# One explicit order of single-engine pieces for the first stage of an attention, MoE and MLP kernel

## The chip, the core and the metric

The kernel runs on one core of a Trainium2 chip. A core has five engines that run side by side, each with its own instruction list in fixed order: PE (TensorE, the matmuls; PEld is its weight load), DVE (VectorE), ACT (ScalarE), POOL (GpSimd) and SP (SyncE, which here only issues DMAs). They wait for each other through semaphores. SBUF is the on-chip memory of 128 partitions; PSUM takes the results of PE. The metric is the device time of one execution in microseconds (us), the median of several runs.

## The reference

```
def _attn_ref(q, k, v, n_global, n_local):
    scores = scale * np.matmul(q, k.transpose(0, 1, 3, 2))
    ...
    scores = np.where(keep, scores + bias, -1e9)   # local window and a few global keys
    a = np.exp(scores - max); a = a / (sum(a) + 1e-09)
    return np.matmul(a, v)

def _moe_ref(x, w_in, w_out, g_ln):
    h = x @ w_in
    e = np.exp(h - max(h)); sm = e / (sum(e) + 1e-09)
    solu = h * sm
    ln = (solu - mean) / np.sqrt(var + 1e-06) * g_ln
    return ln @ w_out

def _moe2_ref(x, w_in, w_out):
    h = x @ w_in
    return (h * (1.0 / (1.0 + np.exp(-h)))) @ w_out
```

Attention has 2 batches, 8 heads, 768 positions and heads of 64; n_global is 8 and n_local 96. Its output, 1536 tokens by 512, goes through the first block (512 to 1024 to 512) and the second (512 to 2048 to 512). The weights arrive as 64-bit floats.

## The kernel before

**Tiles and stages.** The tokens are cut into 12 tiles of 128, six to a batch. The first stage takes each tile through attention and the first block; its result lies transposed in x2T (128 partitions, 4 parts of the model width, 1536 tokens). The second stage takes two groups of 768 tokens through the second block: `up` (L485) and `down` (L512), 16 steps each, interleaved by one.

A tile's chain in the first stage: scores of 8 heads in two groups of four (`scores`, L248); per head the maximum with the bias on DVE (L264), which leaves the biased scores in a tile A and the maximum in negmax, and the exponential on ACT (L265), which also sums into sm; per group the reciprocals of the sums on DVE (L270, L271); a scaling of A by head (`norm`, L115 through the helper `scaled`) on POOL or DVE; eight transposes (L285) and a copy out to ath; the product with v (L304), which lands as a high part xT on ACT (L324) and a low part on DVE (L329); two halves of the product with w_in (L343). Then a softmax times h and a layernorm in pieces lm, le, lu, ls, sq, lc, ld (L353 to L388, the last a scaling of e on POOL), transposes of e (L398), high and low part lnh on ACT (L402) and lnl on DVE (L405), and the product with w_out (L418) for pairs of tiles in two halves, copied to x2T (L428, L430). Tiles of the first position of a batch (0 and 6) have a window of 128 keys, the others 256.

**High and low parts.** Products with weights are made of three: high by high, low by high and high by low. A weight therefore needs a high part and the remainder, and is unpacked first from its 64-bit form, in 48 units of 128x512: load (`cl`, L108, 512 KB, into cx), exponent scaling into cc (`ca`, `cap`, `cav` for ACT, POOL, DVE; L113 or L115), three bit operations on DVE (c1, c2, c3: L128, L130, L132), for w_out a scaling with the gain g_ln (L141, two instructions on POOL), the high copy (L113 on ACT, L115 on DVE) and the subtraction of the low part (L143, POOL). Units 0 to 7 are w_in, 8 to 15 w_out, 16 to 47 the second block.

**Order.** Nothing is scheduled by a compiler: each engine's list is the order in which the program calls the pieces. For tiles 0 to 7 a string START of tokens such as `ea:0` gives it, for tiles 8 to 11 the string STEADY is repeated with the tile number relative, then LAST, and a tail in Python with the first two `up` steps. One token covers several instructions, often on several engines: `ea` is the maxima of two heads on DVE and their exponentials on ACT, `na` and `nb` are the sums of one group (DVE) and its four norms, divided among POOL and DVE by the digit, `cs` is gain, high and low part of a unit. In the repeated part and behind it, `bg` runs a unit's next steps, one unit behind the other. All DMAs are issued by SP.

**Buffers.** cx and cc have 3 buffers, sm 3, st 2 and xT 2 (LEAD). The outputs of `down` are copied from PSUM into a pool tile ob of 6 buffers and sent from there (L519 to L524).

Of the kernel before, what the change touches and what calls it, by code (L numbers as in the profile page):

```python
# [8 lines left out]
F32 = mybir.dt.float32  # L9
# [36 lines left out]
def kernel(ctx, tc, q, k, v, n_global, n_local, w_in, w_out, g_ln, w2_in, w2_out, out):  # L46
# [58 lines left out]
    def u_load(i):  # L105
        src, b, _, _ = units[i]
        x = cv.tile([128, 512, 2], I32, tag="cx", name="cx", bufs=3)
        nc.sync.dma_start(out=x.rearrange("p (b n) t -> p b n t", b=b) if b else x, in_=src)  # L108
        ustate[i] = [x]
# [24 lines left out]
    def u_split(i, eng=None, heng=None):  # L134
        _, b, dest, g = units[i]
        hi, lo = dest()
        w = ustate.pop(i)[1]
        if b:
            w = w.rearrange("p (b n) -> p b n", b=b)
        for j in range(b if g is not None else 0):  # L140
            nc.gpsimd.tensor_scalar(out=w[:, j], in0=w[:, j], scalar1=g[:, j:j + 1], scalar2=1.0, op0=ALU.mult, op1=ALU.mult)  # L141
        scaled(hi, w, heng)
        (eng or nc.gpsimd).tensor_tensor(out=lo, in0=w, in1=f(hi), op=ALU.subtract)  # L143

    NW1 = 2 * KD + KF
    ustep = [NW1 - 3]
# [104 lines left out]
    def softmax(t, qd, j):  # L251
# [3 lines left out]
        if j == 0:  # L255
# [4 lines left out]
        for a in range(2):  # L260
            h, c = 4 * qd + 2 * j + a, 2 * a + j
            bb = bias[:, h, s:s + 2, :].rearrange("p w n -> p (w n)") if tb else bias0[:, h, :]
            m = negmax[:, t * H + h:t * H + h + 1]
            nc.vector.tensor_tensor_reduce(out=x[:, c, 0:n], in0=p[:, a, j, 0:n], in1=bb, scale=-0.125, scalar=1e30, op0=ALU.add, op1=ALU.min, accum_out=m)  # L264
# [570 lines left out]
```

## Time and profile before

| | us |
|---|---|
| median of 3 runs (lowest, highest) | 542.16 (541.45, 544.44) |
| the profiled execution | 541.32 |
| its span, first to last instruction | 539.2 |

| engine | busy us | share of the span | instructions |
|---|---|---|---|
| PE | 496.1 | 92% | 3025 |
| PEld | 436.4 | 81% | 3025 |
| DVE | 316.5 | 59% | 711 |
| ACT | 240.5 | 45% | 548 |
| POOL | 154.5 | 29% | 199 |

The mean granted TensorE clock was 0.988 of full speed. The same page shows the span in 40 slices of 13.5 us, each digit the busy share in tenths (row PEclk is the granted clock):

```profile
PE   1668778899999999989999999999999999999994
PEld 1345657788898889879989899898998999989893
DVE  4998989666645643673988889884263122131221
ACT  3656666456555654544564544543242222122221
POOL 1787885322144314341344333232000000000000
PEclk9998899999999999999999999999999999999997
```

The prediction reads three more views. In the table of windows, a row is a stretch of the span with the busy time of each engine, the granted clock and what the DMAs moved. In the chain of waits, a row is the start, the length and the work that the end of the span depended on at that time. In the groups of instructions, a row has a line, its engine, what it writes and reads with the shapes, the count, the busy time in us with the mean of one in ns, and behind the bar the idle time of the engine just before and what ended it. In the trace, matmuls of scores (L248) and with v (L304) are recorded twice each.

### The profile page before, as it was taken

The numbers are of one execution on the slowest core, as the hardware profiler recorded it, in microseconds if no ns is written. First come the engines' busy times: TensorE is split into PE (matmuls) and PEld (weight loads), VectorE is DVE, ScalarE is ACT, GpSimd is POOL, SyncE is SP. The second block draws the span as 40 slices with busy tenths as digits, with TensorE's granted clock in tenths as the row PEclk, the third lists the DMA queues.
The fourth block names the chain that finished last, engine by engine and source line by source line (L and its number), as shares of the span: only waits on it lengthen the run. The fifth ranks groups of instructions, "written<-read, shape, count | busy, mean of one in ns | idle before, by whom it ended". The sixth has DMA issues, their size and how long they took to land.

```text
span 539.2 us, 8089 instructions
## 1 busy us (share of the span) xinstructions
PE 496.1 (92%) x3025; PEld 436.4 (81%) x3025; DVE 316.5 (59%) x711; ACT 240.5 (45%) x548; POOL 154.5 (29%) x199
## 2 busy tenths in 40 slices
PE   1668778899999999989999999999999999999994
PEld 1345657788898889879989899898998999989893
DVE  4998989666645643673988889884263122131221
ACT  3656666456555654544564544543242222122221
POOL 1787885322144314341344333232000000000000
PEclk9998899999999999999999999999999999999997
DMA  7575430202053000210253342420030000000003
GB/s 210 179 203 170 133 119 23 79 22 78 1 176 98 2 2 1 78 40 1 79 194 119 117 147 98 146 78 2 0 118 1 1 0 1 0 1 1 0 1 123
DMA packets 27487, 38.36 MB, mean 71 GB/s; under 512 B 2864, under 2 KB 15152, under 8 KB 27440
## 3 DMA queue, kind: packets, MB, share of 16 engines
q1 hardware_dynamic: 27440, 37.76, 22.2%
q8 instruction: 26, 0.43, 0.3%
q14 instruction: 21, 0.17, 0.1%
HBM read 34.61 MB, written 3.15 MB: 70 GB/s over the span
## 4 chain that ended last, share of the span: by engine, by line
PE 75%; DVE 9%; POOL 7%; DMA 3%; ACT 3%; issue 2%; SPq 0%; POOLq 0%; ACTq 0%
PE p L485 25%; PE p L512 25%; PE p L418 10%; PE p L343 7%; PE p L285 2%; PE p L248 2%; DMA cx<-in_moe_w_in_dram 2%; PE p L304 2%; PE p L398 2%; POOL A L115 2%; DVE cc L130 1%; DVE cc L132 1%; DVE A L264 1%; POOL cc L141 1%; ACT A L265 1%
## 5 line engine op out<-in xcount | busy, mean ns | idle before, releaser
L494 DVE SCALAR_TENSOR_TENSOR e<-e,p 128x384 f32<-128x384 f32 x64 | 32.6, 550 | 123.8 <-ACT e L491 123.8
L491 ACT ACTIVATE e<-p 128x384 f32<-128x384 f32 x64 | 27.9, 488 | 126.4 <-PE p L485 126.4
L512 PE MATMUL p<-w3h,gl 128*128 128x512 f32 x192 | 75.8, 395 | 0.0
L512 PE MATMUL p<-w3l,gh 128*128 128x512 f32 x192 | 75.7, 394 | 0.0
L512 PE MATMUL p<-w3h,gh 128*128 128x512 f32 x192 | 75.5, 393 | 0.0
L132 DVE SCALAR_TENSOR_TENSOR cc<-cx,cc 128x512 uint32<-128x512 uint32 x48 | 61.3, 1276 | 0.2
L485 PE MATMUL p<-x2h,w2h 128*128 128x384 f32 x256 | 55.6, 338 | 0.0
L485 PE MATMUL p<-x2l,w2h 128*128 128x384 f32 x256 | 55.5, 338 | 0.0
L485 PE MATMUL p<-x2h,w2l 128*128 128x384 f32 x256 | 55.4, 338 | 0.0
L343 PE MATMUL p<-wih,xT 128*128 128x512 f32 x192 | 50.9, 408 | 1.4 <-DVE xT L329 1.4
L265 ACT ACTIVATE A<-A,negmax 128x256 f32<-128x256 f32 (+1 forms) x96 | 45.9, 480 | 13.8 <-DVE negmax L264 12.4
L115 POOL TENSOR_SCALAR A<-A,sm 128x256 f32<-128x256 f32 (+1 forms) x63 | 33.4, 544 | 53.9 <-DVE sm L271 52.4
L485 PEld LDWEIGHTS p<-x2h,w2h 128*128 128x128 f32 x256 | 46.1, 188 | 2.6
L485 PEld LDWEIGHTS p<-x2l,w2h 128*128 128x128 f32 x256 | 46.0, 188 | 0.0
L485 PEld LDWEIGHTS p<-x2h,w2l 128*128 128x128 f32 x256 | 45.8, 188 | 0.0
L343 PEld LDWEIGHTS p<-wih,xT 128*128 128x128 f32 x192 | 35.1, 192 | 10.8 <-issue 1.8
L512 PEld LDWEIGHTS p<-w3h,gl 128*128 128x128 f32 x192 | 36.1, 188 | 8.3
L285 PE MATMUL p<-ident,A 128*128 128x128 f32 x176 | 27.4, 300 | 15.9 <-POOL A L115 15.8
L512 PEld LDWEIGHTS p<-w3l,gh 128*128 128x128 f32 x192 | 36.0, 188 | 7.3
L512 PEld LDWEIGHTS p<-w3h,gh 128*128 128x128 f32 x192 | 36.1, 188 | 7.1
L95 ACT ACTIVATE gh<-e 128x384 fp32r<-128x384 f32 x64 | 31.6, 526 | 20.7 <-DVE e L494 20.7
L130 DVE SCALAR_TENSOR_TENSOR cc<-cx,cc 128x512 uint32<-128x512 uint32 x48 | 39.8, 829 | 0.1
(101 smaller groups left out, 834.0 us busy)
## 6 DMA issues: line engine op xcount, KB each, us to landing
cx<-in_moe_w_in_dram SPq DMA_DIRECT2D x24, 512.0 KB, 3.7
cx<-in_moe_w_out_dram SPq DMA_DIRECT2D x24, 512.0 KB, 3.5
rq<-in_q_dram SPq DMA_DIRECT2D x12, 256.0 KB, 3.9
rk<-in_k_dram SPq DMA_DIRECT2D x12, 256.0 KB, 4.6
vf<-in_v_dram SPq DMA_DIRECT2D x12, 256.0 KB, 4.1
out_dram<-ob SPq DMA_DIRECT2D x12, 256.0 KB, 3.1
ints<-in_n_local_dram SPq DMA_DIRECT2D x1, 1.0 KB, 2.5
ints<-in_n_global_dram SPq DMA_DIRECT2D x1, 1.0 KB, 3.9
```

The costliest lines, as they stand in the source:

```text
L95: nc.scalar.activation(out=hi, in_=src, func=ACTF.Copy)
L115: eng.tensor_scalar(out=out, in0=in_, scalar1=scale, scalar2=1.0, op0=ALU.mult, op1=ALU.mult)
L130: V.scalar_tensor_tensor(out=y, in0=x[:, :, 0].bitcast(U32), scalar=29, in1=y, op0=ALU.logical_shift_right, op1=ALU.bitwise_or)
L132: V.scalar_tensor_tensor(out=y, in0=x[:, :, 1].bitcast(U32), scalar=0x80000000, in1=y, op0=ALU.bitwise_and, op1=ALU.bitwise_or)
L265: nc.scalar.activation(out=x[:, c, 0:n], in_=x[:, c, 0:n], func=ACTF.Exp, bias=m, scale=-1.0, accum_out=sm[:, 0, c:c + 1])
L285: nc.tensor.transpose(p[:, w, o:o + 128], x[:, c, w * 128:(w + 1) * 128], ident)
L343: nc.tensor.matmul(p[:, half, :], lhsT=x[:, a, kk, :], rhs=w[:, kk, n], start=(i == 0), stop=(i == 11))
L418: nc.tensor.matmul(p[:, d], lhsT=x[:, kk, c], rhs=y[:, kk, sl], start=(i == 0), stop=(i == 3 * KF - 1))
L485: nc.tensor.matmul(p, lhsT=w[m // 2][:, kk, c], rhs=x[:, kk, s * HG:(s + 1) * HG], start=(i == 0), stop=(i == 11))
L491: nc.scalar.activation(out=e, in_=p2[:, s, 0:HG], func=ACTF.Tanh, scale=0.5)
L494: nc.vector.scalar_tensor_tensor(out=E[s], in0=E[s], scalar=1.0, in1=p2[:, s, 0:HG], op0=ALU.add, op1=ALU.mult)
L512: nc.tensor.matmul(o, lhsT=x[:, c], rhs=w[m // 2][:, m % 2, :], start=(m == 0 and i == 0), stop=(last and i == 2))
```

## The change

START, STEADY, LAST and the tail give way to one string ORDER of 861 tokens, which covers the first stage from its first load to the last copy into x2T. Its tokens are pieces of one engine, and each names its engine where there is a choice: `d0` to `d7` is the maximum of one head (DVE, now L294), `x0` to `x7` the exponential of one head (ACT, L300), `ra` and `rb` the sums of a group (DVE, L304, L305), `m0p` or `m0v` the norm of one head on POOL or DVE, `oaa` or `oav` the copy out of transposes on ACT or DVE, `ugp`, `uha`, `ulp` (or with v) the gain, high and low part of a unit, `Y00v` one copy into x2T. The head of the table, and the pieces that the old tokens fall into:

```
ORDER = """
cl:0 lq:0 lk:0 cep:0 c1:0 ba:0 sb:0 bb:0 c2:0 cl:1 sa:0 c3:0 d0:0 d4:0 cep:1 d1:0 d5:0 d2:0 lk:1 d6:0 c1:1 d3:0 lq:1 kg:0 c2:1 bc:0 cl:2 d7:0 lq:2
...

-        x = cv.tile([128, 512, 2], I32, tag="cx", name="cx", bufs=3)
-        nc.sync.dma_start(out=x.rearrange("p (b n) t -> p b n t", b=b) if b else x, in_=src)
+        x = cv.tile([128, 512, 2], I32, tag="cx", name="cx", bufs=5)
+        (nc.sync if i else nc.scalar).dma_start(out=x.rearrange("p (b n) t -> p b n t", b=b) if b else x, in_=src)
...
-        c = cv.tile([128, 512], F32, tag="cc", name="cc", bufs=3)
+        c = cv.tile([128, 512], F32, tag="cc", name="cc", bufs=4)
...
-            sm = at.tile([128, 2, 4], F32, tag="sm", name="sm", bufs=3)
+            sm = at.tile([128, 2, 4], F32, tag="sm", name="sm", bufs=6)
...
-        x = m1.tile([128, 2, 4, 128], F32R, tag="xT", name="xT", bufs=LEAD)
+        x = at2.tile([128, 2, 4, 128], F32R, tag="xT", name="xT", bufs=3)
...
-        st = m1.tile([128, 8], F32, tag="st", name="st", bufs=2)
+        st = m1.tile([128, 8], F32, tag="st", name="st", bufs=3)
...
+    def u_gain(i, eng):
+        w, g = u_parts(i)[0], units[i][3]
+        for j in range(units[i][1]):
+            eng.tensor_scalar(out=w[:, j], in0=w[:, j], scalar1=g[:, j:j + 1], scalar2=1.0, op0=ALU.mult, op1=ALU.mult)
+
+    def u_hi(i, eng=None):
+        w, hi, _ = u_parts(i)
+        scaled(hi, w, eng)
+
+    def u_lo(i, eng):
+        w, hi, lo = u_parts(i)
+        eng.tensor_tensor(out=lo, in0=w, in1=f(hi), op=ALU.subtract)
+        ustate.pop(i)
...
-    ustep = [NW1 - 3]
+    NWA = NW1 + 8
+    ustep = [NWA]
...
+    def masks3():
         nc.vector.tensor_copy(bias[:, :, 2, :], bias[:, :, 0, :])
...
+    def snorm(t, i, eng):
+        n = 256 if t % TB else 128
+        qd, _, _, _, c = head(i)
+        x, sm, _ = A[t, qd]
+        scaled(x[:, c, 0:n], x[:, c, 0:n], eng, sm[:, 1, c:c + 1])
...
-                    y = wo.tile([128, DM], F32, tag="ob", name="ob", bufs=6)
+                    y = x2T[:, r // 384, r // 128 % 3 * DM:(r // 128 % 3 + 1) * DM]
...
-        nc.sync.dma_start(out=gt, in_=g_ln.rearrange("(k p) -> p k", p=128))
-        for x in START.split():
+        for x in ORDER.split():
...
+            if x == "lk:0":
+                nc.sync.dma_start(out=gt, in_=g_ln.rearrange("(k p) -> p k", p=128))
```

The pool wo is gone: a result of `down` is copied into a part of x2T that no later step reads, and sent from there. The units of the second block that `bg` runs in the second stage begin with unit 24 instead of continuing two units behind; the split of unit 23 falls into the second stage. The second stage's order is otherwise as it was, with `up` cut into its pieces.

Three places of the order, row by row.

PE around the first product with w_out. Before, the transposes of tile 2's e stand ahead of the first L418 (lnh, lnl by woh, wol), and six groups of products with w_in (L343, 12 matmuls each) lie ahead of these rows:

```order
L398 MATMUL p<-ident,e 128x128 x8
L285 MATMUL p<-ident,A 128x128 x8
L248 MATMUL p<-rk,rq 128x256 x4
L418 MATMUL p<-lnh,woh 128x256 x8
L418 MATMUL p<-lnh,wol 128x256 x8
L418 MATMUL p<-lnl,woh 128x256 x8
```

The first L398 of these rows is that of tile 1; the one of tile 2 stands fourteen rows on. In the changed kernel the same engine reads, with L380 for the products with w_in, L275 for scores, L341 for the product with v and L455 for that with w_out:

```order
L380 MATMUL p<-wil,xT 128x512 x4
L275 MATMUL p<-rk,rq 128x128 x4
L341 MATMUL p<-ath,vf 64x128 x16
L455 MATMUL p<-lnh,woh 128x256 x8
L455 MATMUL p<-lnh,wol 128x256 x8
L455 MATMUL p<-lnl,woh 128x256 x8
```

Ten groups of products with w_in now lie ahead of the first L455, and scores of tile 6 (128 wide) and a product with v moved ahead of it.

DVE at the end of tile 1's second softmax group. Before, the sums (L270, L271) are followed at once by two norms of A, and by bit operations of one weight unit (L128, L130, L132):

```order
L270 TENSOR_SCALAR sm<-sm 128x4
L271 RECIPROCAL sm<-sm 128x4
L115 TENSOR_SCALAR A<-A,sm 128x256 x2
L130 SCALAR_TENSOR_TENSOR cc<-cx,cc 128x512
L132 SCALAR_TENSOR_TENSOR cc<-cx,cc 128x512
L128 TENSOR_SCALAR cc<-cc 128x512
```

In the changed kernel, with L294 for the maxima, L304 and L305 for the sums and L139, L141, L143 for the bit operations:

```order
L304 TENSOR_SCALAR sm<-sm 128x4
L305 RECIPROCAL sm<-sm 128x4
L294 ISA A,negmax<-p,bias 128x256
L294 ISA negmax 128x1
L143 SCALAR_TENSOR_TENSOR cc<-cx,cc 128x512
L141 SCALAR_TENSOR_TENSOR cc<-cx,cc 128x512
```

The norms left DVE's list here and stand on POOL's; a maximum and the bit operations of two units follow the sums.

The start. Before, SP issues every load, the first weight unit (cx) as the sixth:

```order
L570 DMA ints<-in_n_local_dram 128x2
L571 DMA ints<-in_n_global_dram 128x2
L573 DMA gt<-in_moe_g_ln_dram 128x8x1
L174 DMA rq<-in_q_dram 128x4x128
L174 DMA rk<-in_k_dram 128x4x128
L108 DMA cx<-in_moe_w_in_dram 128x1024
```

In the changed kernel ACT's list begins with that load, ahead of its table load and the scalings that make the bias:

```order
L119 DMA cx<-in_moe_w_in_dram 128x1024
L124 ACT_TABLE_LOAD
L124 ACTIVATE bias_92<-dm 128x128 x8
L124 ACTIVATE bias<-dm 128x256 x8
L300 ACTIVATE A,sm<-A,negmax 128x128 x8
```

The first weight load left SP's queue for ACT's; on SP, q and k now follow the two integers directly, and gt stands behind k.

More of the change, by code (lines that the diff above doesn't have):

```diff
@@ L132, in u_bits, with u_parts, u_split @@
             V.scalar_tensor_tensor(out=y, in0=x[:, :, 1].bitcast(U32), scalar=0x80000000, in1=y, op0=ALU.bitwise_and, op1=ALU.bitwise_or)
-    def u_split(i, eng=None, heng=None):
-        _, b, dest, g = units[i]
+    def u_parts(i):
+        _, b, dest, _ = units[i]
         hi, lo = dest()
[L137 to L143, printed above, removed]
+        w = ustate[i][1]
+        return (w.rearrange("p (b n) -> p b n", b=b) if b else w), hi, lo
+    def u_gain(i, eng):
[9 more added lines that the diff above has]
+        ustate.pop(i)
+    def u_split(i):
+        u_hi(i)
+        u_lo(i, nc.gpsimd)
     NW1 = 2 * KD + KF
-    ustep = [NW1 - 3]
+    NWA = NW1 + 8
+    ustep = [NWA]
     def bg(n=1, limit=None):
@@ L249, in scores, with head, smax @@
         A[t, qd] = p
-    def softmax(t, qd, j):
+    def head(i):
+        qd, j, a = i // 4, i // 2 % 2, i % 2
+        return qd, j, a, 4 * qd + 2 * j + a, 2 * a + j
+    def smax(t, i):
         tb = t % TB
@@ L420, in x2, with x2_out @@
         x2p[t, half] = p, s1 > s0
-    def x2_out(t, half, act=True):
-        p, up = x2p.pop((t, half))
-        for j in range(2):
-            tt = t + j if up else t + 1 - j
-            o = x2T[:, 2 * half:2 * half + 2, tt * 128:(tt + 1) * 128]
-            if act:
-                nc.scalar.activation(out=o, in_=p[:, :, j], func=ACTF.Copy)
-            else:
-                nc.vector.tensor_copy(o, p[:, :, j])
-    def step(fn):
-        def go(t):
-            if t:
-                fn(t - 1 if t % 2 else t - 2, (t + 1) % 2)
-        return go
+    def x2_out(t, half, j, eng=None):
+        p, fwd = x2p[t, half]
+        tt = t + j if fwd else t + 1 - j
+        scaled(x2T[:, 2 * half:2 * half + 2, tt * 128:(tt + 1) * 128], p[:, :, j], eng)
     for half in range(2):
@@ L469, with x2_hi, x2_lo, up_mm @@
             unit(w2ow[r:r + 128, :, :], 0, lambda i=i, j=j: (w3h[i][:, j], w3l[i][:, j]))
+    def x2_hi(g, kk):
+        nc.scalar.activation(out=x2h[:, kk], in_=x2T[:, kk, g * G:(g + 1) * G], func=ACTF.Copy)
+    def x2_lo(g, kk):
+        nc.vector.tensor_tensor(out=x2l[:, kk], in0=x2T[:, kk, g * G:(g + 1) * G], in1=f(x2h[:, kk]), op=ALU.subtract)
     def x2split(g):
         for kk in range(KD):
[L473 removed]
+            x2_hi(g, kk)
+            x2_lo(g, kk)
     gs = {}
[L477 removed]
+    def up_mm(g, m):
         c = slice((m % 2) * 128, (m % 2) * 128 + 128)
@@ L486, in up, with up_act, up_mul, up_hi @@
                     i += 1
-        E, R = [], range(2)
-        for s in R:
+        gs[g, m] = p2
+    def up_act(g, m):
+        p2 = gs[g, m]
+        for s in range(2):
             e = wk.tile([128, HG], F32, tag="e2", name="e2", bufs=2)
-            gs[g, m, s] = [wk.tile([128, HG], F32R, tag=x, name=x, bufs=4) for x in ("gh", "gl")]
+            gs[g, m, s] = [e] + [wk.tile([128, HG], F32R, tag=x, name=x, bufs=4) for x in ("gh", "gl")]
             nc.scalar.activation(out=e, in_=p2[:, s, 0:HG], func=ACTF.Tanh, scale=0.5)
-            E.append(e)
-        for s in R:
-            nc.vector.scalar_tensor_tensor(out=E[s], in0=E[s], scalar=1.0, in1=p2[:, s, 0:HG], op0=ALU.add, op1=ALU.mult)
-        for s in R:
-            hilo(E[s], *gs[g, m, s])
+    def up_mul(g, m):
+        p2 = gs.pop((g, m))
+        for s in range(2):
+            e = gs[g, m, s][0]
+            nc.vector.scalar_tensor_tensor(out=e, in0=e, scalar=1.0, in1=p2[:, s, 0:HG], op0=ALU.add, op1=ALU.mult)
+    def up_hi(g, m):
+        for s in range(2):
+            e, hi, _ = gs[g, m, s]
+            nc.scalar.activation(out=hi, in_=e, func=ACTF.Copy)
+    def up_lo(g, m):
+        for s in range(2):
+            e, hi, lo = gs[g, m, s]
+            nc.vector.tensor_tensor(out=lo, in0=e, in1=f(hi), op=ALU.subtract)
+            gs[g, m, s] = hi, lo
+    def up(g, m, nbg=0):
+        up_mm(g, m)
+        up_act(g, m)
+        up_mul(g, m)
+        for s in range(2):
+            e, hi, lo = gs[g, m, s]
+            hilo(e, hi, lo)
+            gs[g, m, s] = hi, lo
         bg(nbg)
@@ L569 @@
+    for h in range(2):
+        for j in range(2):
+            OPS[f"Y{h}{j}a"] = lambda p, h=h, j=j: x2_out(2 * p, h, j)
+            OPS[f"Y{h}{j}v"] = lambda p, h=h, j=j: x2_out(2 * p, h, j, V_)
     with tc.manual_schedule():
```

184 lines of the change are left out of this document (77 added, 107 removed).

## The prediction

> **What bounds the kernel now.** I read the table of windows first, cut where the character of the work changes: the front, the rest of the first stage, the second stage, the end.
>
> ```profile
> core 0: us, PE busy (x) PEld busy (x) DVE busy (x) ACT busy (x) POOL busy (x), PEclk, DMA share, GB/s
> 0.00:104.08 104.08, 70.77 (x463) 53.19 (x463) 85.36 (x240) 59.77 (x159) 67.89 (x95) 0.97 0.48 144
> 104.08:270.85 166.77, 164.86 (x1267) 148.42 (x1268) 98.63 (x271) 89.73 (x209) 49.08 (x79) 1.00 0.16 49
> 270.85:531.38 260.53, 260.49 (x1297) 234.77 (x1295) 131.84 (x201) 90.39 (x182) 37.56 (x26) 1.00 0.16 54
> 531.38:539.20 7.82, 0.00 (x0) 0.00 (x0) 0.69 (x1) 0.59 (x1) 0.00 (x0) 0.62 0.41 147
> ```
>
> From 104.08 to 531.38 us PE is busy all but 1.9 us (166.77 - 164.86). Nothing that frees another engine there can shorten it; only PE arriving earlier at that place can. Before 104.08 PE is not the bound: DVE works 85.36 of 104.08 us and PE's 70.77 are drawn out by waits between matmuls. How much PE time the front loses, the chain of waits tells, in the stretch where PE runs without a gap. There one tile costs
>
> ```profile
> 161.05 1.93 PE p L248 x16
> 162.98 2.98 PE p L343 x12
> 165.96 1.90 PE p L304 x32
> 167.86 5.94 PE p L418 x48
> 173.80 0.87 PE p L398 x8
> 174.68 1.75 PE p L285 x16
> 176.42 2.75 PE p L343 x12
> ...
> 254.92 4.17 PE p L485 x24
> ```
>
> 18.12 us: scores (L248), products with w_in (L343), with v (L304), with w_out (L418), transposes (L398, L285). Twelve tiles are 217.4; the first tile of each of the two batches has half the scores, transposes and value products, (1.93 + 1.75 + 1.90) / 2 = 2.8 less, so 5.6; two blocks of L485 of 4.17 end the stage, 8.3. Together 220.1 us of dense work by 270.85. Of it 164.9 lie behind 104.08, so by 104.08 PE had done only 220.1 - 164.9 = 55.2 us of work: **48.9 us are lost in the front, and 1.9 behind it**. The change can gain only from the 48.9.
>
> Who loses them, the view of waits tells for the front (total, times, longest), with the DVE and POOL groups of the front:
>
> ```profile
> PE p L285 <- POOL A L115: 15.8, 11, 4.8
> PE p L248 <- DMA rk<-in_k_dram: 7.2, 1, 7.2
> DVE sm L270 <- ACT A L265: 4.4, 3, 3.2
> DVE cc L115 <- DMA cx<-in_moe_w_in_dram: 2.3, 1, 2.3
> ```
>
> ```profile
> L130 DVE SCALAR_TENSOR_TENSOR cc<-cx,cc 128x512 uint32<-128x512 uint32 x16 | 13.5, 847 | 0.1
> L132 DVE SCALAR_TENSOR_TENSOR cc<-cx,cc 128x512 uint32<-128x512 uint32 x16 | 13.1, 822 | 0.2
> L128 DVE TENSOR_SCALAR cc<-cc 128x512 uint32<-128x512 uint32 x16 | 10.0, 624 | 1.1 <-POOL cc L115 1.1
> L115 DVE TENSOR_SCALAR A<-A,sm 128x256 f32<-128x256 f32 x19 | 9.1, 532 | 0.2
> L364 DVE CUSTOM_DVE_ANT_0 e<-p,e 128x1024 f32<-128x1024 f32 x3 | 3.6, 1216 | 0.0
> L329 DVE TENSOR_TENSOR xT<-p,xT 128x512 fp32r<-128x512 f32 x5 | 3.4, 677 | 0.0
> L115 DVE TENSOR_SCALAR cc<-cx 128x512 f32<-128x512 f32 x3 | 3.3, 1093 | 2.3 <-DMA cx<-in_moe_w_in_dram 2.3
> L264 DVE CUSTOM_DVE_ANT_0 A<-p,bias 128x128 f32<-128x128 f32 x8 | 2.0, 283 | 0.0
> L115 DVE TENSOR_SCALAR wih<-cc 128x512 fp32r<-128x512 f32 x3 | 1.4, 458 | 0.0
> ```
>
> ```profile
> L115 POOL TENSOR_SCALAR A<-A,sm 128x256 f32<-128x256 f32 x21 | 13.4, 651 | 2.9 <-ACT xT L324 1.5 <-DVE sm L271 1.4
> L143 POOL TENSOR_TENSOR wol<-cc,woh 128x512 fp32r<-128x512 f32 x8 | 11.3, 1413 | 5.6 <-ACT woh L113 4.5 <-DVE woh L115 0.5 <-DVE sm L270 0.5
> L388 POOL TENSOR_SCALAR e<-e,st 128x1024 f32<-128x1024 f32 x3 | 4.1, 1358 | 0.3
> ```
>
> PE's longest waits end with POOL's norm of A, but POOL itself waits for the sums of DVE, and DVE is busy four fifths of the time, 36.6 us of it (13.5 + 13.1 + 10.0) with the three bit operations of the 16 weight units, all of which come ahead of the first L418. So **DVE's list of work ahead of the first L418 sets the front**.
>
> **The new order, counted to the same place.** Before, PE's chain closes at the L398 of tile 2 (about 104.7 us), 55.2 us of work plus half a us behind it; DVE has then done the bit operations of all 16 units. In the new order the place with the same property is the second block of L455 (the second half of the first pair's product with w_out): all 16 units are needed there too. What stands ahead of it in the order listings, against before:
>
> - PE: 8 small scores (half of the 1.93 that eight wide ones take, which the trace counts twice: 1.0) and 4 wide ones (1.0), 20 transposes (2.19 at 1.75 per 16), a value product (1.90), three halves of w_in (3 x 2.87, the mean of 2.98 and 2.75) and two transposes of e (2 x 0.87). That is 2.0 + 2.2 + 1.9 + 8.6 + 1.7 = **16.4 us more PE work already done**, 72.1 in all.
> - DVE loses 18 of 20 norms (18 x 0.532 = 9.6), its 3 exponent scalings (3 x 1.093 = 3.3; POOL or ACT do them) and its 5 hi copies (5 x 0.458 = 2.3): 15.2 less. It gains 8 small head maxima (2.0), two xT subtractions (2 x 0.677 = 1.35), one more tile of layernorm and its lo part (three passes over 1024 elements at 1.216 = 3.65, and small column work, estimated at 0.8), two gains (priced as a norm of the same 128x256, 2 x 0.532 = 1.1) and two lo subtractions (priced as L329, 2 x 0.677 = 1.35): 10.2 more. **DVE needs 5.0 us less** there, though it stands ahead of more PE work.
> - POOL takes 22 of the norms more (22 x 0.651 = 14.3) and one more e (1.4), loses two of 16 lo subtractions (2 x 1.413 = 2.8): **12.9 more, 81 us** instead of 67.9.
>
> POOL's load has a price on DVE. Where both work, the bit operations are longer than next to an idle POOL:
>
> ```profile
> 17.02 0.35 DVE cc L128
> 17.39 0.70 DVE cc L130
> 18.12 0.69 DVE cc L132
> ```
>
> 1.74 us a unit against 0.847 + 0.822 + 0.624 = 2.29 in the mean of the front, where POOL was busy 0.65 of the time. If the excess of 0.55 goes with POOL's share and that rises to about 0.80, it is 0.13 a unit more, 16 units: **2.0 us back**. Its bounds are wide. With no growth it is 0. In the second stage one of the three operations takes
>
> ```profile
> L132 DVE SCALAR_TENSOR_TENSOR cc<-cx,cc 128x512 uint32<-128x512 uint32 x25 | 40.0, 1602 | 0.0
> ```
>
> 1.602, so 16 x (1.602 - 0.822) = 12.5 us is the other end. I take 2.0, as the front's own rows are the nearest.
>
> **The first load on ACT's queue.** Before it stood sixth on SP:
>
> ```profile
> 3.29 1.70 SPq L108 DMA_DIRECT2D cx<-in_moe_w_in_dram  x1
> ...
> 7.15 1.70 ACT L113 ACTIVATE bias<-dm 128x128 bf16<-128x128 f32 x8 [5.13 <-DVE dm L209]
> ```
>
> Now it is ACT's first instruction, at about 0.7, ahead of ACT's table load; ACT idles 5.13 us up to 7.15, which hides issue and table load. SP loses this issue (1.70) and takes gt, one issue, behind the first q and k. DVE waited 2.3 us for this load, so 2.3 is the most it can win. Its 512 KB now run beside q and k, and PE's first wait (7.2, for rk) can grow; how much, the trace doesn't show, but not by more than those 2.6 us by which the load comes earlier. DVE works weights before scores there, so I take **1.0**, bounds 2.3 and -0.3. The Trainium skill (DMA: Bandwidth & Descriptors, section "Issuing engines are not separate DMA queues") says that loads issued by different engines share the same 16 DMA engines, and that only the issuing time is saved. By it nothing is transferred faster, the term stays under 1.70, and the sum would be at most 0.7 lower in us; the traces of before have no second issuer to test it.
>
> **Edits at nothing.** More buffers for cx, cc, sm, st and xT add no instruction; they let the order run ahead, which the counts contain. The staged results are the same copies and DMAs with another address; they must follow the last split of x2T, which stands ahead of them on the same two engines. Splitting the bias copy moves one copy under half a us. The second-stage units come one later: some 3 us of DVE work go from the first stage to the second, where DVE is busy 131.84 of 260.53 us, so PE hides it; without that cover it costs 3 us. The second stage and the end keep their 260.5 and 7.8.
>
> **Sum.** The closing place comes at 104.7 - 5.0 + 2.0 - 1.0 = 100.7 us with 72.1 + 0.5 us of work done, so 28.1 us lost instead of 48.9. With the 1.9 behind it kept, the gain is 20.8, of which I take 20, since small bookkeeping operations are left out. The profiled execution took 541.32 us (span 539.2 and 2.1 around it), 0.15% below the median of the three runs, 542.16; on its base the forecast is **521.3 us**.
>
> **Rivals.**
>
> 1. *DVE also waits less.* DVE idles 104.08 - 85.36 = 18.7 us in the front, 9.8 of them up to its first weights. The single-engine pieces put other work into waits such as the 4.4 us for ACT's exponentials. If nearly all of the 9 us behind the start go, the time is 521.3 - 9 = 512. For it: the order is free at each piece. Against: buffers and the softmax chain (max, exp, sum, norm) remain. 0.14.
> 2. *POOL takes over.* 81 us of work, a start at 7.2, and waits of 15 to 20 us (it idled 36 us before) give the closing place at 103 to 108: 31 to 36 us lost, a gain of 13 to 18, so about 526. For it: PE's largest wait already ends with POOL, and DVE's norms go there. Against: its work is now interleaved finer. 0.20.
> 3. *The front is latency, not load.* If PE stays behind the same chain through ACT and POOL and the extra PE work only moves behind the bound, nothing changes: 541. For it: 15.8 us of waits for the norms. Against: 85.36 us of DVE work in 104. 0.04.
> 4. *Slower: PE's clock.* The denser front has short bursts and gaps.
>
> ```profile
> 9.50:14.00 4.50, 0.00 (x0) 0.00 (x0) 4.07 (x18) 1.76 (x8) 1.58 (x3) 1.00 0.86 313
> 14.00:20.00 6.00, 3.39 (x12) 1.87 (x12) 5.90 (x18) 4.69 (x17) 3.12 (x6) 1.00 0.31 95
> ...
> 58.00:61.00 3.00, 3.00 (x34) 2.57 (x31) 2.96 (x10) 2.19 (x8) 2.26 (x3) 0.64 0.28 100
> ```
>
> Its granted clock was 0.97 in the front's mean but 0.64 for three us after a gap at 55 to 58. 72.6 us of work from 7.2 on at clock c end at 7.2 + 72.6 / c; the break-even with 48.9 lost is 121.5, so c = 0.635. At 0.55 the place comes at 139 and the time is 541.3 + (139 - 121.5) = 559. It decides only below 0.635 over the whole front. 0.04. The Trainium skill (TensorE: Matmul & The Clock Gate, section "Part 1: The HAM clock gate (the "warmup" mystery)") says that an idle window of about 3.4 us halves the clock until as long a busy one has passed; the trace agrees at 58 (0.64) and not at 14, where 4.5 idle us were followed by 1.00. By the rule every gap of the front would cost, and the time would come out near 541 only if they were as many as its bursts.
>
> **How the numbers follow.** The forecast, 516 to 524, has 0.56; the rivals have 0.14, 0.20, 0.04 and 0.04, and 0.02 is left. The range reaches from rival 1 (512) to the upper half of the unknown costs: the bit operations at the second stage's price would put it at 521.3 + 10.5 = 532. So 511 to 533. A measurement of this kernel tells about 0.5% from no change: faster by more is 0.91 (forecast, rivals 1 and 2, and part of the rest), within 0.04, slower 0.05.
>
> **What would show it.** Right: the second L455 block starts near 101 us, from there PE runs without gaps; PE's loss before it is near 28; DVE has few norms (L126 on A) in the front, POOL is busy some 80 us by then; the second stage is still 260.5. Wrong: bit operations at over 2.6 us a unit; PE waits behind 110 us; POOL without idle time ahead of the closing place (rival 2); a granted clock below 0.8 in the front (rival 4); PE's first scores later than 9 us.

## The result and the profile after

| | before | after |
|---|---|---|
| median, us (4 runs each; lowest, highest) | 542.85 (541.45, 544.44) | 527.70 (527.44, 528.66) |
| ratio after / before, 95% interval | | 0.9723 (0.9691 to 0.9755) |
| profiled execution, us (span) | 541.32 (539.2) | 527.69 (525.6) |

The change made the kernel 15.1 us faster by the medians and 13.6 by the two profiled executions. The forecast was 20 us, 521.3, with a range of 511 to 533.

The first view is the table of windows, cut alike for both kernels: start and length of the stretch, then the busy time of PE, PEld, DVE, ACT and POOL, the granted clock, and the DMAs. First after, then before.

```profile
core 0: us, PE busy (x) PEld busy (x) DVE busy (x) ACT busy (x) POOL busy (x), PEclk, DMA share, GB/s
0.00:40.00 40.00, 22.17 (x128) 16.22 (x128) 27.35 (x96) 25.47 (x79) 24.36 (x42) 0.87 0.73 219
40.00:105.00 65.00, 64.22 (x474) 52.00 (x473) 55.36 (x155) 47.41 (x112) 53.22 (x77) 1.00 0.41 122
105.00:220.00 115.00, 115.00 (x875) 99.91 (x874) 77.55 (x233) 61.53 (x142) 32.23 (x53) 1.00 0.19 58
220.00:230.00 10.00, 6.53 (x55) 6.32 (x54) 7.79 (x12) 3.14 (x5) 8.18 (x5) 1.00 0.14 52
256.81:517.70 260.89, 260.65 (x1298) 234.91 (x1296) 129.85 (x199) 90.26 (x180) 36.59 (x25) 1.00 0.14 47
```

```profile
0.00:40.00 40.00, 19.63 (x97) 13.39 (x98) 31.21 (x87) 21.02 (x64) 23.73 (x38) 1.00 0.67 197
40.00:105.00 65.00, 52.05 (x376) 40.72 (x375) 54.81 (x155) 38.75 (x96) 44.16 (x59) 0.95 0.36 110
...
270.69:531.38 260.69, 260.65 (x1298) 234.93 (x1296) 132.00 (x201) 90.55 (x182) 37.72 (x26) 1.00 0.16 54
```

The gain lies in one stretch. From 40 to 105 us PE was idle 12.95 us before (65 - 52.05) and is idle 0.78 now. In the first 40 us it was idle 20.4 and still is 17.8. Behind 105 it lost 1.9 before and loses 3.5 now, between 220 and 230. The second stage is 260.9 against 260.7. So (20.4 - 17.8) + (12.95 - 0.78) - (3.5 - 1.9) - 0.2 = 13.0 of the 13.6 us.

Idle time does not count that a busy matmul may be drawn out. So I also price the matmuls done by a time, from their counts by shape in the trace and the chain's rows (1.93 us per 16 records of a wide score, 1.75 per 16 transposes, 1.90 per 32 with v, 2.75 per 12 with w_in, 0.87 per 8 transposes of e, 5.75 per 48 with w_out), and call the rest of the time lost. By 40 us before has lost 29.5 and after 28.7; by 105 us 50.0 and 33.8. The expectations below use these two numbers.

PE's idle time is 33.3 us of the 50.0 and 18.6 of the 33.8, so the gain is nearly all idle time. The rest, 16.7 and 15.2 us, is matmuls that last longer than their price, some 9 and 11 of it in the first 40 us. There the same work takes nearly twice as long as later, as the scores show in the timeline of after:

```profile
21.58 1.66 PE L275 MATMUL p<-rk,rq 64*128 64x256 f32 x8
28.99 2.08 PE L275 MATMUL p<-rk,rq 64*128 64x256 f32 x8
43.91 1.13 PE L275 MATMUL p<-rk,rq 64*128 64x256 f32 x8
```

The row of the granted clock does not tell all of it: from 20 to 25 us it reads 1.00. No experiment below was aimed at this part.

The place that the forecast named, the second L455 block, in the timeline of after (start, length, engine, line, operands):

```profile
102.67 1.09 PE L435 MATMUL p<-ident,e 128*128 128x128 f32 x8
103.52 1.20 PE L455 MATMUL p<-lnh,woh 128*128 128x256 f32 x8
```

It starts at 103.5, not at 100.7. (Before, the place to compare it with is the L398 of tile 2 at 104.7, which stands behind the first L418, at 90.2; ahead of that one stand the transposes of tile 1's e.) The groups of DVE and POOL ahead of it (count, busy time, mean in ns, idle before):

```profile
L143 DVE SCALAR_TENSOR_TENSOR cc<-cx,cc 128x512 uint32<-128x512 uint32 x16 | 13.4, 845 | 0.1
L141 DVE SCALAR_TENSOR_TENSOR cc<-cx,cc 128x512 uint32<-128x512 uint32 x16 | 12.9, 814 | 0.2
L139 DVE TENSOR_SCALAR cc<-cc 128x512 uint32<-128x512 uint32 x16 | 9.2, 577 | 1.6 <-POOL cc L126 1.1 <-ACT cc L124 0.3
```

```profile
L126 POOL TENSOR_SCALAR A<-A,sm 128x256 f32<-128x256 f32 x39 | 24.9, 651 | 6.9 <-DVE sm L305 4.0 <-ACT A L300 3.0
L162 POOL TENSOR_TENSOR wol<-cc,woh 128x512 fp32r<-128x512 f32 x7 | 10.5, 1507 | 0.0
```

The three bit operations take 2.24 us a unit, not the 2.42 that the forecast allowed. DVE is busy 81.3 us by then and POOL 76.8.

The start, from the timeline of after:

```profile
0.73 0.41 ACTq L119 DMA_DIRECT2D cx<-in_moe_w_in_dram  x1
...
3.22 3.75 SPq L119 DMA_DIRECT2D cx<-in_moe_w_in_dram  x1
...
7.02 0.17 DVE L226 CAST nlf<-ints 128x4 f32<-128x4 int32 x1 [4.75 <-DMA ints<-in_n_global_dram]
...
9.26 0.42 DVE L139 TENSOR_SCALAR cc<-cc 128x512 uint32<-128x512 uint32 x1
```

The weights are there early (first bit operation 9.26, before 10.29), but n_global lands at 7.02 instead of 5.19, SP's next load takes 3.75 us to issue instead of 0.50, and PE's first scores start at 9.0 instead of 7.2. The late loss, from the view of waits and the timeline:

```profile
PE p L435 <- POOL e L425: 3.5, 1, 3.5
```

```profile
221.71 4.48 POOL L420 TENSOR_TENSOR st<-st,mhalf 128x1 f32<-128x1 f32 x1 [10.87 <-DVE st L419]
...
222.22 3.55 DVE L501 TENSOR_TENSOR x2l<-x2T,x2h 128x768 fp32r<-128x768 f32 x4
```

L420 works on one column and takes about 0.56 us elsewhere. Here it lasts until DVE's four subtractions are done.

### The profile page after: what moved, and what is told of

Same layout as the page of the kernel before. It is cut to its first block, busy times and chain, and to the rows that moved or that the text cites. A ratio compares the mean times of both kernels' runs of the same rounds, so it can differ in the third digit from the quotient of the medians.

```text
span 525.6 us, 8114 instructions
## 1 busy us (share of the span) xinstructions
PE 495.4 (94%) x3025; PEld 436.1 (83%) x3025; DVE 311.9 (59%) x721; ACT 236.4 (45%) x532; POOL 157.7 (30%) x205
## 4 chain that ended last, share of the span: by engine, by line
PE 88%; DVE 4%; POOL 3%; issue 2%; SPq 1%; DMA 1%; ACT 0%; DVEq 0%; POOLq 0%
PE p L518 26%; PE p L569 25%; PE p L455 12%; PE p L380 10%; PE p L275 4%; PE p L322 4%; PE p L341 4%; PE p L435 2%; DMA rq<-in_q_dram 1%; POOL st L420 1%; DVE A L294 1%; POOL A L126 1%; SPq L119 1%; POOL e L425 1%; DVE st L390 0%
## 5 line engine op out<-in xcount | busy, mean ns | idle before, releaser
L143 DVE SCALAR_TENSOR_TENSOR cc<-cx,cc 128x512 uint32<-128x512 uint32 x48 | 58.5, 1221 | 0.2
L300 ACT ACTIVATE A<-A,negmax 128x256 f32<-128x256 f32 (+1 forms) x96 | 46.2, 483 | 14.3 <-DVE negmax L294 13.9
L380 PE MATMUL p<-wih,xT 128*128 128x512 f32 x192 | 50.7, 406 | 0.0
L126 POOL TENSOR_SCALAR A<-A,sm 128x256 f32<-128x256 f32 (+1 forms) x71 | 40.5, 582 | 31.1 <-DVE sm L305 25.9
L294 DVE CUSTOM_DVE_ANT_0 A<-p,bias 128x256 f32<-128x256 f32 (+1 forms) x96 | 34.8, 395 | 16.9 <-PE p L322 6.3
L380 PEld LDWEIGHTS p<-wih,xT 128*128 128x128 f32 x192 | 34.5, 189 | 9.0 <-issue 1.7
L275 PE MATMUL p<-rk,rq 64*128 64x256 f32 (+1 forms) x192 | 29.6, 441 | 11.2 <-DMA rk<-in_k_dram 9.0
L162 POOL TENSOR_TENSOR w3l<-cc,w3h 128x512 fp32r<-128x512 f32 x16 | 23.5, 1468 | 52.0 <-ACT w3h L124 48.6
```

Source lines behind the costliest of these rows:

```text
L126: eng.tensor_scalar(out=out, in0=in_, scalar1=scale, scalar2=1.0, op0=ALU.mult, op1=ALU.mult)
L143: V.scalar_tensor_tensor(out=y, in0=x[:, :, 1].bitcast(U32), scalar=0x80000000, in1=y, op0=ALU.bitwise_and, op1=ALU.bitwise_or)
L162: eng.tensor_tensor(out=lo, in0=w, in1=f(hi), op=ALU.subtract)
L275: nc.tensor.matmul(p[:, a, j, 0:128 * len(ks)], lhsT=rq[z, t % 2, pr, :], rhs=rk[z, W, pr, :], start=True, stop=True)
L300: nc.scalar.activation(out=x[:, c, 0:n], in_=x[:, c, 0:n], func=ACTF.Exp, bias=negmax[:, t * H + h:t * H + h + 1], scale=-1.0, accum_out=s ...
L380: nc.tensor.matmul(p[:, half, :], lhsT=x[:, a, kk, :], rhs=w[:, kk, n], start=(i == 0), stop=(i == 11))
```

## The experiments

The theory to test was the forecast's: DVE's list sets the front, so relief of DVE is what gains. The rivals: POOL sets it; the order of the pieces does; or the arrival of the loads.

**1. The first load back on SP.**

```
-cl:0 lq:0 lk:0 cep:0 c1:0
+lq:0 lk:0 cl:0 cep:0 c1:0
-        (nc.sync if i else nc.scalar).dma_start(...)
+        nc.sync.dma_start(...)
```

> The changed kernel with the first weight load back on SP, behind the first q and k as before. Theory of the forecast (DVE works weights first, so the earlier load wins 1.0 us): the time rises by about 1.0 to 528.7 us, the first bit operation on DVE starts near 10.5 us instead of 9.3. Rival (the 512 KB beside q, k and n_global delay the mask, the first scores and the loads of tile 1): n_global lands near 5.2 us instead of 7.0, the first scores start near 7.2 instead of 9.0, SP's next weight load is issued in under 2 us instead of 3.75, and the time falls by 1 to 2, to 526 us.

Measured: 529.73 us, ratio to before 0.9771 (0.9744 to 0.9799), 2.0 above the changed kernel, with intervals that overlap. Its timeline:

```profile
5.09 0.17 DVE L226 CAST nlf<-ints 128x4 f32<-128x4 int32 x1 [2.83 <-DMA ints<-in_n_global_dram]
...
10.43 0.43 DVE L139 TENSOR_SCALAR cc<-cc 128x512 uint32<-128x512 uint32 x1 [3.02 <-POOL cc L126]
```

The time rose, as in the theory. Both sides of the trade are there: the mask 1.9 us earlier, the first bit operation 1.2 later. In the front they cancel: the loss by 105 us is 33.9 against 33.8, and the second L455 block starts at 103.7. In this profile the extra time lies elsewhere: behind the late wait the clock falls, which it did not do in the profile of after. Two rows of this run, then one of after:

```profile
227.00:230.00 3.00, 0.43 (x3) 0.43 (x4) 1.16 (x1) 0.00 (x0) 2.89 (x4) 0.96 0.00 0
230.00:233.00 3.00, 3.00 (x16) 3.00 (x15) 0.52 (x1) 1.58 (x2) 0.75 (x1) 0.50 0.00 0
```

```profile
230.00:233.00 3.00, 3.00 (x28) 3.00 (x27) 1.43 (x2) 2.12 (x3) 0.56 (x1) 1.00 0.00 0
```

So moving the load is worth at most 2 us, and the trace does not show that the front gains any of it.

This bears on most of what follows. The profiles of the new order in experiments 2 and 4 to 8 have the same late wait of 3.5 us, and in each the clock is 0.50 to 0.57 in the three us behind it; over six us it is 0.50 to 0.77, which is 1.4 to 3.0 us of work. Only the profile of after shows 1.00. Small differences in time to after are therefore not those of the front alone, and the loss by 105 us is the better measure of the front.

**2. Norms back on DVE, in the new order.** 19 tokens of tiles 0 to 5, such as:

```
-... m3p:0 ... m6p:1 ... m7p:1 ...
+... m3v:0 ... m6v:1 ... m7v:1 ...
```

> The changed kernel with 19 norms of tiles 0 to 5 moved from POOL back to DVE, at the same places of the order. Theory (DVE's list sets the front): about 19 x 0.53 = 10 us more on DVE ahead of the second L455 block, so it starts near 113 us and the time is 534 to 538 us. Rival 1 (POOL sets the pace): POOL has 12 us less, the time is 520 to 526. Rival 2 (neither list but the chain through the engines): within 2 us of 527.7.

Measured: 531.55 us, 0.9795 (0.9768 to 0.9822): 3.9 us for 10 us more on DVE, between the theories. The loss by 105 us is 36.3, 2.5 more; the rest goes with the clock behind the late wait. A new wait in the front, among those of PE from 40 to 105 us:

```profile
PE p L322 <- DVE A L126: 2.3, 2, 1.9
```

**3. The new engines in the old order.** In START, for 26 tokens:

```
-cav:0 ... csw:0 ... nb2:1 ... na4:3
+cap:0 ... cs:0 ... nb:1 ... na:3
```

> The kernel before with its own order, where only the engine of 26 pieces differs: all norms of START on POOL, all its exponent scalings on POOL and all its high copies on ACT. DVE loses about 15 us ahead of its first products with w_out. Theory (DVE's list alone sets the front): 526 to 531 us, near the changed kernel. Rival (the gain needs the other order, as PE finds no more work within reach and POOL delays the norms): 537 to 546 us.

Measured: 547.78 us, 1.009 (1.0056 to 1.0125): **5.5 us slower than before (542.25 in the same runs), with 16 us less on DVE by 105 us (69.9, before 86.0)**. That lies above the range of the rival too. Its windows:

```profile
0.00:40.00 40.00, 20.07 (x90) 12.82 (x91) 25.06 (x78) 21.16 (x63) 27.34 (x43) 0.87 0.61 185
40.00:105.00 65.00, 52.71 (x327) 40.78 (x325) 44.87 (x125) 38.68 (x93) 45.48 (x65) 0.84 0.34 101
```

From 40 to 105 us PE does fewer matmuls (327 records against 376), but it does not wait more: by 105 us it is idle 32.2 us, before 33.3. Single waits are longer: those for POOL's norm and for e reach 5.5 and 3.6 us (before 4.8 and 2.0), and POOL itself now waits 7.6 us for high copies on ACT (before 4.5). The view of waits, PE and then POOL:

```profile
PE p L285 <- POOL A L115: 15.4, 12, 5.5
...
PE p L398 <- POOL e L388: 5.6, 2, 3.6
```

```profile
POOL wol L143 <- ACT woh L113: 7.6, 8, 2.2
```

POOL takes its list in order: while it waits for a high copy, the norms behind that stand still too, and here there are more of them. So 16 us less on DVE take 1.1 us off PE's idle time. The loss by 105 us still rises to 55.9, 5.9 more than before, as the granted clock is 0.87 and 0.84 in the two stretches where it was 1.00 and 0.95, and the same busy time of PE holds less work. That the longer single waits bring the clock down is likely, but not shown. Executions of both kernels with a mean clock of 0.978 still differ (547.85 and 549.25 against 543.29 and 543.63), so the clock need not be all of it in every execution.

**4. The old engines in the new order.** Experiment 2, with three exponent scalings (`cev`) and five high copies (`uhv`) on DVE too.

> The changed kernel with the engines of before for the pieces ahead of the first products with w_out: 19 norms, 3 exponent scalings and 5 high copies back on DVE, at their places of the new order. With the kernel before, the changed one and the order of before with the new engines this makes a table of two orders by two engine choices. Theory (the order brings the gain, since PE finds other work at its waits; DVE's load counts for about a quarter of its size, 15 us giving 4): 531 to 535 us, ahead of before by 8 or more. Rival (DVE's list paces the front one to one, as the forecast had it): 15 us more on DVE, 540 to 543 us.

Measured: 530.4 us in the middle of three executions, 0.9783 (0.9742 to 0.9824); a fourth took 2730.66 us and is not in the ratio. PE is idle 21.8 us by 105 us, and the loss is 35.1. With this the table is full (us; the new order comes with its buffers and the first load on ACT):

| | engines of before | engines of after |
|---|---|---|
| order of before | 542.5 | 547.8 |
| order of after | 530.4 | 527.7 |

The order brings 12 us with the old engines and 20 with the new; the engines cost 5 in the old order and bring at most 3 in the new, where the intervals overlap and the loss by 105 us differs by 1.3. Of the 12, the load of experiment 1 can be 2 and the buffers of experiment 8 can be 1.7. Two gains and two subtractions of low parts stay on DVE in the new order, where before had them on POOL.

**5. The bit operations left out, in both orders.**

```
-        if n == 1:
+        if n == 1 and i >= 16:
-        if n == 2:
+        if n == 2 and i >= 16:
```

> The changed kernel without two of the three bit operations (c2, c3) of the 16 weight units of the first stage: 32 DVE instructions, 26.3 us, are left out, so signs and low bits of these weights are missing. Theory 1 (DVE's list still paces the front one to one): PE's loss by 105 us falls by 15 or more, the time to 505 to 512. Theory 2 (in the new order DVE's load counts for a quarter, as 10 to 15 us more of it cost 3 to 4): about 6 us less, 520 to 523. Theory 3 (the loss that is left is the chain of the first tiles): 525 to 528, and the loss by 40 us stays at 27 to 29.

> The kernel before without the same 32 DVE instructions (c2, c3 of units 0 to 15), 26.6 us of its front. Theory of the forecast (DVE's list sets the front of the kernel before): 20 us or more of the 50 lost come back, 515 to 522 us. Rival (what stops PE is that each engine's list holds pieces in a poor order, as taking 15 us off DVE's list made it slower): 532 to 540 us.

Measured: after without them 525.40 us, 0.9691 (0.9671 to 0.9710), 2.3 us less than after; before without them 527.71, 0.9724 (0.9701 to 0.9746), **14.6 us less than before**. Windows of the one, then of the other:

```profile
0.00:40.00 40.00, 22.85 (x146) 17.19 (x147) 20.32 (x82) 27.12 (x83) 23.58 (x48) 0.96 0.74 230
40.00:105.00 65.00, 64.73 (x491) 53.57 (x490) 45.47 (x147) 48.15 (x118) 43.15 (x73) 1.00 0.35 114
```

```profile
0.00:40.00 40.00, 25.09 (x142) 17.78 (x143) 24.48 (x88) 24.57 (x77) 23.16 (x41) 1.00 0.72 225
40.00:105.00 65.00, 58.67 (x448) 48.87 (x448) 47.97 (x154) 41.38 (x105) 35.69 (x59) 0.95 0.31 97
```

Neither of the two expected pictures of the kernel before is right: the 26.6 us of DVE work cost it 14.6 us, 0.55 us each, and PE's idle time by 105 us falls by 12.1. In the new order the same work costs 2.3 us, 0.09 each. That is the time of theory 3, but the loss by 40 us does not stay: it falls to 25.6, and by 105 us to 29.5, 4.3 less or 0.16 us each, of which 1.2 is idle time. The clock behind the late wait, 0.50 for six us here, takes part of it back. The two operations are also the last to read cx, so leaving them out frees its buffers earlier; how much of either gain is due to that stays open.

**6. POOL's norms of tiles 0 to 5 left out.**

```
-        scaled(x[:, c, 0:n], x[:, c, 0:n], eng, sm[:, 1, c:c + 1])
+        if t > 5 or eng is not nc.gpsimd:
+            scaled(x[:, c, 0:n], x[:, c, 0:n], eng, sm[:, 1, c:c + 1])
```

> The changed kernel without POOL's norms of tiles 0 to 5: about 45 POOL instructions, some 27 us ahead of the second L455 block, are left out, so these tiles' attention weights are not divided by their sums. Theory (POOL, 77 us of work by 103 us, sets what loss is left): PE's loss by 105 us falls from 33.8 to 20 or less, the time to 512 to 517. Rival (POOL is only one link): 523 to 527.

Measured: 523.42 us, 0.9653 (0.9634 to 0.9672), 4.3 us less than after for some 27 us less on POOL. POOL is one link too, not the bound. The loss by 40 us is 24.1 and by 105 us 27.2, 6.6 less, but only 0.8 of that is idle time of PE; the rest is matmuls that last less long.

**7. Tile 1's q and k ahead of the second weight load.**

```
-cl:0 lq:0 lk:0 cep:0 ... c2:0 cl:1 sa:0 ... d2:0 lk:1 d6:0 c1:1 d3:0 lq:1 kg:0
+cl:0 lq:0 lk:0 lk:1 lq:1 cl:1 cep:0 ... c2:0 sa:0 ... d2:0 d6:0 c1:1 d3:0 kg:0
```

> The changed kernel with q and k of tile 1 issued ahead of the second weight load on SP (before, that load's issue took 3.75 us and tile 1's q landed at 13.3). Theory (the first 40 us, where 29 us of PE time are lost, hang on when tiles arrive): tile 1's scores start 2 to 3 us earlier, PE's loss by 40 us falls from 28.7 to 26 or less, the time to 525 to 526. Rival (they hang on DVE's bit operations and the softmax chain): loss by 40 us 28 or more, the time 527 to 529.

Measured: 530.71 us, 0.9783 (0.9751 to 0.9814): a miss, and 3 us slower than after. Its timeline, SP and then PE:

```profile
3.22 3.87 SPq L199 DMA_DIRECT2D rk<-in_k_dram  x1
```

```profile
9.33 4.60 PE L275 MATMUL p<-rk,rq 64*128 64x128 f32 x32 [9.33 <-DMA rk<-in_k_dram]
17.86 1.12 PE L322 MATMUL p<-ident,A 128*128 128x128 f32 x4 [3.94 <-POOL A L126]
```

The scores of tile 1 do follow those of tile 0 without the gap of 2.2 us. But PE then waits 3.9 us for the first norm, which comes 0.8 us later than in after. The sixth DMA of SP takes 3.9 us to issue here too, though it is a q and k load now: so that time does not hang on the size of SP's own load. The loss by 40 us is 29.2.

**8. Fewer buffers.**

```
-... name="cx", bufs=5 ... name="sm", bufs=6 ... name="xT", bufs=3 ... name="st", bufs=3
+... name="cx", bufs=4 ... name="sm", bufs=3 ... name="xT", bufs=2 ... name="st", bufs=2
```

> The changed kernel with 4 buffers of cx instead of 5 and the old numbers for sm (3), st (2) and xT (2). Theory (these buffers are what lets pieces run ahead): a loss of 3 to 8 us, 531 to 536. Rival (the order alone carries the gain, buffers beyond what it must have are idle): within 1 us of 527.7.

Measured: 529.43 us, 0.9752 (0.9722 to 0.9782), 1.7 above after with intervals that overlap, between the two. The loss by 105 us is 35.1, 1.3 more. One wait is new in the front:

```profile
PE p L275 <- DMA rk<-in_k_dram: 1.4, 1, 1.4
```

SP waits longer for a free cx, and the k of a later tile stands behind it. Three buffers of cx or of cc were not tried in this order, so how much the further ones are worth stays open.

**9. The end of the first stage, in three orders.** In the first the subtractions x2l are moved behind the low part of tile 10:

```
-xs2:0 uhv:21 xs1:0 xs3:0 X0:4 ... c2:20 yl:10 lu:11 up:0
+xs2:0 uhv:21 X0:4 ... c2:20 yl:10 xs1:0 xs3:0 lu:11 up:0
```

> The changed kernel with the four subtractions x2l (L501, 128x768) moved on DVE behind the low part of tile 10. Theory (POOL's one-column operation L420 of 4.48 us lasts so long because those four run beside it, and it is what PE's last wait of 3.5 us ends with): L420 takes under 1 us there, the wait shrinks to under 1 us, the time is 524.5 to 525.5 us. Rival (tile 10's chain is late for another reason): the wait stays at 2 to 3.5 us, the time at 527 to 528.

Measured: 526.88 us, 0.9704 (0.9674 to 0.9735), 0.8 us less than after with intervals that overlap, between theory and rival. L420 takes 1.00 us now, and tile 10's wait is gone, but x2l stands ahead of tile 11's layernorm, and its transposes wait 2.2 us:

```profile
PE p L435 <- POOL e L425: 2.2, 1, 2.2
```

In the second, tile 11's exponential and passes are called ahead of X0:4 as well:

```
-lm:11 lc:10 c1:23 xs2:0 uhv:21 xs1:0 xs3:0 X0:4 ... yh:10 le:11 c2:20 yl:10 lu:11 up:0 ls:11 sq:11
+lm:11 le:11 lc:10 c1:23 uhv:21 lu:11 ls:11 xs2:0 sq:11 X0:4 ... yh:10 c2:20 yl:10 xs1:0 xs3:0 up:0
```

> The changed kernel with the end of the first stage in another order: tile 11's exponential, its DVE passes lu and ls and its squares stand ahead of the last copies of the pairs, and the four subtractions x2l behind the low part of tile 10. Theory (PE's only wait behind 105 us is the late layernorm chain of the last two tiles): that wait of 3.5 us falls under 0.7 and the time to 523.5 to 525 us. Rival (up 0 then waits for x2l, or another wait takes its place): 526.5 to 528.

Measured: 528.34 us, 0.9727 (0.9694 to 0.9760): the rival. The waits for e are gone, the first `up` step waits for x2l instead, and the clock falls to 0.77 behind these short waits:

```profile
PE p L518 <- DVE x2l L501: 1.8, 4, 0.7
```

```profile
230.00:245.00 15.00, 13.23 (x65) 11.90 (x64) 9.50 (x15) 4.59 (x9) 2.55 (x4) 0.77 0.11 36
```

In the third, x2l takes the idle time of DVE right behind the first copy of pair 4, when POOL is done with tile 10:

```
-lm:11 lc:10 c1:23 xs2:0 uhv:21 xs1:0 xs3:0 X0:4 ulp:22 Y00v:4 ld:10 yt:10 X1:4 yh:10 le:11 c2:20 yl:10 lu:11 up:0 ls:11 sq:11 c3:20 ... c2:23 lc:11 pt:0 pg:0 ld:11
+lm:11 lc:10 c1:23 xs2:0 uhv:21 X0:4 ulp:22 Y00v:4 ld:10 yt:10 le:11 xs1:0 xs3:0 lu:11 ls:11 X1:4 yh:10 sq:11 yl:10 lc:11 ld:11 c2:20 up:0 c3:20 ... c2:23 pt:0 pg:0
```

> The changed kernel with the end of the first stage in a third order: the four subtractions x2l stand on DVE behind the first copy of pair 4, so beside no POOL work of tile 10 and ahead of the first up step's need, and tile 11's layernorm right behind them. Theory (PE's 3.5 us wait and the clock drop behind such waits are all that is lost late): no PE wait over 0.7 us behind 105 us, granted clock 1.00 from there, the time 523 to 524.5 us. Rival (another wait takes its place, as with the two orders tried): 526 to 528.

Measured: **523.56 us, 0.9648 (0.9623 to 0.9673)**, 4.1 us less than after and the fastest version that leaves nothing out.

```profile
220.00:230.00 10.00, 10.00 (x85) 9.92 (x84) 6.35 (x11) 5.60 (x9) 3.61 (x4) 1.00 0.16 52
230.00:245.00 15.00, 15.00 (x107) 14.96 (x106) 13.01 (x23) 6.10 (x12) 5.34 (x5) 1.00 0.22 70
```

PE has no idle time behind 105 us and the clock stays at 1.00.

## Why the forecast came out as it did

- **Where the time is lost: right.** Only the front had time to give. The second stage kept its 260.7 us.
- **More PE work ahead of the closing place: right in kind, a little too large.** 16.4 us were counted; the order has 12 more transposes there, not 20, so it is 15.5. This was nearly the whole gain, and it is what experiment 4 leaves in place.
- **The step that failed: "DVE's list of work ahead of the first L418 sets the front".** It was read off a busy share of four fifths. In the order of before, DVE's work did cost 0.55 us per us (experiment 5), but giving 16 us of it to POOL and ACT took only 1.1 us off PE's idle time and made the kernel slower (experiment 3). In the new order DVE's work costs 0.09 us per us left out, and 0.2 to 0.4 per us added (experiments 2 and 4); by the loss at 105 us it is 0.16, and 0.1 to 0.25. The term that rested on it, 5.0 us less on DVE, 2.0 back by contention and 1.0 for the load, was to bring the closing place 4.0 us earlier; it came 1.2 earlier. DVE did get 4.6 us lighter (81.3 us by 103.5, before 85.9 by 104.7), but its idle time grew by 3.5: 22.3 against 18.8.
- **Contention of the bit operations: a wrong sign.** They cost 2.24 us a unit beside a busier POOL, before 2.29.
- **The first load: the 1.0 is not shown to be wrong, its place is.** The weights came 1.0 earlier, as forecast; the mask and the scores paid for it with 1.8 us, inside the 2.6 that were kept as a bound. The first scores start at 9.0 us, right at the mark that the forecast gave as a sign of being wrong.
- **The waits behind: mis-sized.** 1.9 us were kept; 3.5 were measured, through POOL's L420 beside x2l. Nothing in the forecast looked at this edge, though the order there was rewritten too. "PE waits behind 110 us" was one of its own signs of being wrong.
- **The 48.9 us lost: not all waits.** The forecast had PE's 70.77 us "drawn out by waits between matmuls". By 105 us a third of what is lost, 16.7 of 50.0, is the matmuls themselves, and the change left 15.2 of that in place. For the same reason the reading of the clock at 14 us is wrong: the row says 1.00, but the eight records of a wide score at 15.8 us take 2.08 us, those at 89.1 take 1.13. So that gap is no case of a full clock behind a long wait.
- **A term that was missing.** Where scores, transposes and other kinds alternate on PE in smaller pieces, these pieces cost more: two halves of a tile's scores that stand apart take 1.06 us each, together they were 1.93 in before; two halves of its transposes 1.03 each (0.87 at other places) against 1.75. That is up to 0.5 us a tile. Other pieces got a little shorter (w_in 2.81 us where 2.87 was the mean), and why the small ones cost more is not shown.

Rows of the chain of after, records as in before:

```profile
132.30 1.06 PE p L275 x8
133.37 1.03 PE p L322 x8
```

Summed: 541.3 - 1.2 - 15.5 + 1.6 (waits) leaves 526.2, and the 1.5 us left to 527.7 are put down to the pieces and to 0.3 of the second stage and end. That the forecast was within 6.4 us is partly luck: the order term carried it, while the DVE term behind it was mostly not there.

**Rivals.** POOL as the new pace (526) hit the number but not the cause: 27 us less on POOL gives 4.3 us. Nothing gained did not happen, and the clock decided nothing for this change (0.87 up to 40 us and 1.00 up to 105, before 1.00 and 0.95); in experiment 3 it did. What is left of the loss is in the first 40 us, 24 to 29 us in every version of the new order (before 29.5), with less on DVE, less on POOL or other loads. 17 to 20 us of it are idle time, which belongs to the chain of the first tiles, max, exponential, sum, norm, transposes; that no single engine bounds this chain is argued from experiments 5 to 7, not shown. The other 6 to 11 us are matmuls that take up to twice their later time. What it would take to shorten either was not tried.

## What to carry to other kernels

An engine that is busy 80% of a stage is a suspect, not the bound: leave out a part of its work and see how much of it comes back, in the old and in the new order. Where engines run their lists in order, what counts is which independent work stands at each wait; moving 16 us to less busy engines without a new order took 1.1 us off PE's idle time here. Set the time of a matmul against that of the same shape elsewhere in the trace: a busy PE can be a slow one, and idle time alone hides it. And look at the edges of a rewritten order too: one wait of 3.5 us late in the stage, with the clock behind it, cost a quarter of the gain and was removed by moving some ten tokens.

## What the hardware showed that was not expected

A one-column POOL operation of 0.56 us took 4.48 us beside four DVE subtractions with two inputs from SBUF, and 1.00 us when these were moved away. The Trainium skill (SBUF — State Buffer, section "SBUF: two separate sides") says that such a DVE operation and a POOL operation that reads SBUF share a port pair as an exclusive lock, which the one that starts first holds for its instruction. The trace agrees that POOL is blocked. It was blocked through all four, though it had started at 221.71 and the first of them at 222.22; DVE was in a bit operation at that moment (L139, from 221.56), and whether that one held the pair is not shown.

A wait of PE of some 3 us can cost half as much again or more: behind the same 3.5 us wait the granted clock fell to 0.50 to 0.57 for 3 us or longer in seven profiles of the new order, and not at all in that of after, so kernels that are alike there can differ by 1.4 to 3.0 us. The Trainium skill (TensorE: Matmul & The Clock Gate, section "Part 1: The HAM clock gate (the "warmup" mystery)") has a window of about 3.4 us that runs free of the program; that the same wait is followed by a drop in most runs and by none in another fits that. In experiment 9 a wait of 2.2 us was followed by 0.58 over three us in the first order, and four waits of at most 0.7 us by 0.77 over 15 us in the second. What brought the clock down there, no run shows.

A DMA issue on one queue took longer beside a large load on another: SP's sixth issue took 3.75 and 3.87 us behind ACT's 512 KB (after and experiment 7), against 1.70 in before and 2.39 for two loads in experiment 1, both with that load on SP. A load of 1 KB landed 1.8 us later beside it.
